# Half-height low passes in the first product of a two-layer MoE chain behind agent attention, with new ranks for the planner

## The chip, the cores and the metric

One Trainium2 chip, of which the kernel uses one core. Its engines are TensorE (PE, with its weight loads PEld), VectorE (DVE), ScalarE (ACT), GpSimd (POOL) and SyncE (SP), which here only issues DMAs. The metric is the device time of the kernel in microseconds (us), the median of three runs; lower is better.

## What is computed

The input is 12480 tokens of 128 numbers. Agent attention (49 agents) is followed by two pairs of dense layers, each 128 to 2048 to 128 wide, all in float32:

```python
def sm(a, b):
    s = scale * (a @ b.transpose(0, 2, 1))
    s = s - s.max(-1, keepdims=True)
    e = np.exp(s)
    return e / (e.sum(-1, keepdims=True) + 1e-09)
x = sm(q, agents) @ (sm(agents, k) @ v)      # attention through the agents
h = x @ w_in                                 # first pair: a rational function
P = a[0] + a[1] * h + a[2] * h**2 + a[3] * h**3
Q = 1.0 + abs(b[0]) * abs(h) + abs(b[1]) * h**2
x = (P / (Q + 1e-6)) @ w_out
h = x @ w2_in                                # second pair: a squared ReLU
x = (s * np.maximum(h, 0)**2 + b2) @ w2_out
```

## The kernel before

The kernel first goes over the keys and values in 13 blocks and reduces them to 49 agent vectors; with w_in these are multiplied into a matrix of 49 x 2048, "avw". Its high and low parts (fp32 split into two fp32r numbers) lie in `avwh` and `avwl`, each with the agents' rows twice: at partitions 0 to 48 and at 64 to 112. The weights are converted from a packed 64-bit form meanwhile (`conv_...`).

The main part goes over the tokens in 24 tiles of 512 and one of 192. For a tile, the scores of its queries on the agents are made (`q_...` jobs), and their softmax is transposed into `pt`: rows 0 to 48 hold the high parts of the 49 weights, rows 64 to 112 the low parts. The 2048 hidden columns are 16 chunks of 128; a **unit** is two chunks of one tile, so a tile of 512 has eight units and there are 196 units in all, numbered p. A unit of the first pair takes these steps:

- `m1_h(p, k)`, for k = 0 and 1 (L681, PE): chunk k of h into a PSUM bank, as a pass of `avwh` and a pass of `avwl` over all rows of `pt`. The bank of k = 0 is one of two, that of k = 1 the middle one, which every unit uses;
- `m1_z` and `m1_abs` (ACT, both as L326, into `z_all` and `t_all`), `m1_w` (POOL, L696 and L698, into `w_all`), `m1_u2` and `m1_u3` (DVE, L702 and L705);
- `m1_ln` and `m1_exp` (ACT), `m1_e` and `m1_m` (DVE, L717 and L721), then either `m1_g` (DVE, L731) or, for units in `ADD_POOL`, `m1_a` and `m1_ga` (POOL, L725 and L728);
- `m1_out` (PE, L739): the product with w_out into one accumulator.

When a tile has all its units, the second pair follows per unit: `m2_h` (PE, three fp32r passes for each of the two chunks, L762 to L764, through one bank `bb`), `m2_relu` (ACT), a square (`m2_sqa` on ACT for units in `SQ_ACT`, else `m2_sqp` on POOL, L773) and `m2_out` (PE, L777).

Nobody orders these by hand. A planner (`main_jobs`, `in_order`) lists all jobs with an engine, a booked time, what must be over before and a rank, which is the unit's number plus a constant of the job's kind (`RANK`); the second pair's unit number is moved back by `BEHIND` behind its tile's end. It then runs a list schedule: on each engine the job of lowest rank among those that are ready, or will be within `PATIENCE`. The program issues each engine's instructions in that fixed order. In main_jobs, the booked times of POOL are `w * 0.00352` for `m1_w`, `w * 0.0019 + 0.05` for a square, `w * 0.00117 + 0.07` for `m1_a` and `w * 0.00233` for `m1_ga`, with w = 1024. `SLOTS` gives the number of buffers of each kind.

Of the kernel before, what the change touches and what calls it, by code (L numbers as in the profile page):

```python
# [20 lines left out]
P = 128  # L21
NA = 49
# [22 lines left out]


W_ACT = {4, 10, 13}
ADD_POOL = {p for p in range(12, NU - 4) if p % 8 in (1, 5)}
SQ_ACT = {p for p, (_, j) in enumerate(OF_UNIT) if j in (0, 2, 4, 6) or p > NU - 5}

# [1 line left out]
SLOTS = dict(own=2, mid=1, r=1, b=1, acc0=1, acc1=1, z=2, t=2, w=4, u=6, l=4, g=4, v=3, xh=2, xl=2, pt=2, qt=2,  # L54
             ss=2, pp=2, mx=2, sr=2, cv=2)
OFFSET = dict(w=2, u=2, v=2, t=1)
SCORES, TRANS, BEHIND = 14, 8, 4


RANK = dict(h=-1.38, z=1.18, abs=0.03, y=3.05, w=4.62, u2=0.32, u3=-3.45, ln=4.31, exp=4.82, e=9.95,  # L60
            m=6.52, g=18.73, a=-0.17, ga=-0.92, out=-0.39, hi=-3.64, lo=4.56, m2h=9.73, relu=0.83,
            sq=9.28, m2out=12.05, evac=4.14, q=-0.25, conv=3, avw=0)

# [2 lines left out]
SAME = dict(pe=0.0, act=0.145, dve=0.127, pool=0.1, sp=0.0)  # L68
FREE = dict(pe=1.3, act=0.0, dve=1.2, pool=3.7, sp=0.0)
COLD = 0.0  # L70
PATIENCE = dict(pe=0.26, act=0.2, dve=0, pool=0.22, sp=0.0)


def act_us(w, psum=True, pointers=0):
# [11 lines left out]
def pe_us(passes, columns, chunks, floor=0.0025):  # L86
    return passes * (columns / 2400 + chunks * floor)


def main_jobs():  # L90
# [43 lines left out]
    for i, n in enumerate(TILES):  # L134
# [19 lines left out]
        for j in range(UNITS[i]):  # L154
            p = f + j
            hs, z, t = [("own", p), ("mid", p)], ("z", p), ("t", p)
            wb, u, l, r, g = ((tag, p) for tag in "wulrg")
            for k in range(2):
                cs = range((2 * j + k) * cpb, (2 * j + k + 1) * cpb)
                need = [("q_pt", i)] if i else [("avw_lo", c // 2 if c < 4 else 1 + c // 4) for c in cs]  # L160
                add(("m1_h", p, k), "pe", pe_us(2, w / 2, cpb, 0.0175), p, "h", need, [hs[k], ("pt", i)])
            hj = [("m1_h", p, k) for k in range(2)]
            add(("m1_z", p), "act", act_us(w, pointers=2), p, "z", hj, hs + [z])
            add(("m1_abs", p), "act", act_us(w), p, "abs", hj, hs + [t])
            if p in W_ACT:
                add(("m1_y", p), "act", act_us(w, False, 2), p, "y", [("m1_abs", p)], [t, wb])
                add(("m1_w", p), "pool", w * 0.00233, p, "w", [("m1_y", p)], [t, wb])
            else:
                add(("m1_w", p), "pool", w * 0.00352, p, "w", [("m1_abs", p)], [t, wb])

            add(("m1_u2", p), "dve", dve_us(w), p, "u2", [("m1_z", p), ("m1_abs", p)], hs + [z])
            add(("m1_u3", p), "dve", dve_us(w, 1), p, "u3", [("m1_u2", p)], hs + [z, u])
            add(("m1_ln", p), "act", act_us(w, False), p, "ln", [("m1_w", p)], [wb, l])
            add(("m1_exp", p), "act", act_us(w, False), p, "exp", [("m1_ln", p)], [l, r])
            add(("m1_e", p), "dve", dve_us(w), p, "e", [("m1_exp", p)], [wb, r, g])
            add(("m1_m", p), "dve", dve_us(w), p, "m", [("m1_e", p)], [r, g])
            if p in ADD_POOL:
                add(("m1_a", p), "pool", w * 0.00117 + 0.07, p, "a", [("m1_u3", p)], [u])
                add(("m1_ga", p), "pool", w * 0.00233, p, "ga", [("m1_m", p), ("m1_a", p)], [g, u])
            else:  # L180
                add(("m1_g", p), "dve", dve_us(w, 1), p, "g", [("m1_m", p), ("m1_u3", p)], [r, g, u])
            for k in range(2):
                prior = [("m1_out", p, 0)] if k else [("m1_out", p - 1, 1)] if j else []
                add(("m1_out", p, k), "pe", pe_us(4, w / 2, cpb), p + 1, "out",
                    [("m1_ga" if p in ADD_POOL else "m1_g", p)] + prior,
                    [g, ("acc0", i)])
# [80 lines left out]
def kernel(  # L267
# [57 lines left out]
    def act(out, in_, func, **kw):  # L325
        return nc.scalar.activation(out=out, in_=in_, func=func, **kw)  # L326
# [334 lines left out]
    def q_pt(i):  # L661
        n = TILES[i]
        pts[i] = sm.tile([P, 512], F32R, tag="pt", name=f"pt{i}")[:, :n]
        act(pts[i], qtps.pop(i)[:, :n], AF.Copy)


    acc1, xs = {}, {}
# [5 lines left out]
    def r_view(p):  # L673
        return rb[:, :, :width(OF_UNIT[p][0])]

    def m1_h(p, k):
        x = 1 if k else 2 * slot["own", p]
        for c, o, n in chunks(p, k):
            dst = xb[:, x, o:o + n]
            for first, w in ((True, avwh), (False, avwl)):  # L680
                on_banks(nc.tensor.matmul(out=dst, lhsT=w[:, c * P:(c + 1) * P], rhs=pts[OF_UNIT[p][0]],  # L681
                                          start=first, stop=not first), {x}, "pe")

    def m1_z(p):
        on_banks(act(view("z", p), h_view(p), AF.Identity, scale=a3, bias=a2), banks(p), "act")
# [256 lines left out]
```

## Time and profile before

| | |
|---|---|
| median of three runs | 1358.8 us (1358.78 to 1360.07) |
| profiled execution, its own time | 1357.7 us |
| its span, first to last instruction | 1355.9 us |
| PE busy | 1261.3 us (93%), 4213 instructions |
| DVE busy | 1229.1 us (91%), 1178 |
| ACT busy | 1177.8 us (87%), 1524 |
| POOL busy | 1196.0 us (88%), 701 |
| mean granted TensorE clock | 0.97 |

"Busy" is the time in which an instruction of the engine was running. A matmul's record is longer than the distance to the next one's start, since matmuls are pipelined, so a busy PE need not be a full PE. The span has four parts: the keys (to about 75 us), a start in which first units and weight conversion mix (to about 186 us), the repeating stretch of tiles (to about 1309 us), and a tail with what is left of the second pair.

### The profile page before, as it was taken

The numbers are of one execution on the slowest core, as the hardware profiler recorded it, in microseconds if no ns is written. First come the engines' busy times: TensorE is split into PE (matmuls) and PEld (weight loads), VectorE is DVE, ScalarE is ACT, GpSimd is POOL, SyncE is SP. The second block draws the span as 40 slices with busy tenths as digits, with TensorE's granted clock in tenths as the row PEclk, the third lists the DMA queues.
The fourth block names the chain that finished last, engine by engine and source line by source line (L and its number), as shares of the span: only waits on it lengthen the run. The fifth ranks groups of instructions, "written<-read, shape, count | busy, mean of one in ns | idle before, by whom it ended". The sixth has DMA issues, their size and how long they took to land.

```text
span 1355.9 us, 12969 instructions
## 1 busy us (share of the span) xinstructions
PE 1261.3 (93%) x4213; PEld 719.0 (53%) x4213; DVE 1229.1 (91%) x1178; ACT 1177.8 (87%) x1524; POOL 1196.0 (88%) x701
## 2 busy tenths in 40 slices
PE   5665699999999999999999999999999999999998
PEld 3342355555555555555555555555555555555565
DVE  5879989999999999999999999999999999999880
ACT  3557689899999999999999999999999999999874
POOL 2567878999999999999999999999999999999851
PEclk9768799999999999999999999999999999999999
DMA  8701000000000000000000000000000000000000
GB/s 338 266 24 39 8 0 16 1 16 16 8 8 16 8 8 16 8 8 16 8 8 16 16 0 16 16 8 8 16 8 8 16 4 8 8 0 8 8 8 11
DMA packets 14004, 34.81 MB, mean 26 GB/s; under 512 B 2192, under 2 KB 2672, under 8 KB 13936
## 3 DMA queue, kind: packets, MB, share of 16 engines
q1 hardware_dynamic: 13360, 33.98, 7.1%
q8 instruction: 33, 0.54, 0.2%
q14 instruction: 35, 0.29, 0.1%
q10 hardware_dynamic: 576, 0.00, 0.0%
HBM read 27.59 MB, written 6.39 MB: 25 GB/s over the span
## 4 chain that ended last, share of the span: by engine, by line
POOL 50%; PE 36%; DVE 6%; ACT 4%; issue 3%; DMA 1%; SPq 0%; POOLq 0%; DVEq 0%; ACTq 0%
POOL w_all L698 20%; PE acc L739 13%; POOL w_all L696 10%; POOL g_all L728 8%; PE acc L777 8%; POOL v_all L773 6%; POOL u_all L725 5%; PE xb L681 5%; PE bb L762 3%; ACT t_all L326 2%; PE bb L763 2%; PE bb L764 2%; PE bb L600 1%; DVE z_all L702 1%; ACT z_all L326 1%
## 5 line engine op out<-in xcount | busy, mean ns | idle before, releaser
L698 POOL TENSOR_TENSOR w_all<-w_all,t_all 128x1024 f32<-128x1024 f32 (+1 forms) x196 | 465.4, 2375 | 18.6 <-ACT w_all L326 2.5
L739 PE MATMUL acc<-g_all,wout_sb 128*128 128x512 f32 (+1 forms) x800 | 374.1, 600 | 25.2 <-POOL g_all L728 12.8
L777 PE MATMUL acc<-v_all,w2out_sb 128*128 128x512 f32 (+1 forms) x800 | 379.2, 581 | 0.7 <-POOL v_all L773 0.5
L326 ACT ACTIVATE v_all<-bb 128x512 f32<-128x512 f32 (+1 forms) x392 | 234.9, 599 | 46.2 <-PE bb L764 37.7
L702 DVE TENSOR_TENSOR z_all<-xb,z_all 128x1024 f32<-128x1024 f32 (+1 forms) x196 | 238.3, 1216 | 39.9 <-ACT z_all L326 38.3
L696 POOL TENSOR_SCALAR w_all<-t_all,absb 128x1024 f32<-128x1024 f32 (+1 forms) x193 | 231.3, 1198 | 41.5 <-ACT t_all L326 39.8
L762 PE MATMUL bb<-xh,w2l 128*128 128x512 f32 (+1 forms) x400 | 251.1, 628 | 9.6 <-ACT v_all L326 8.8
L705 DVE SCALAR_TENSOR_TENSOR u_all<-z_all,prm,xb 128x1024 f32<-128x1024 f32 (+1 forms) x196 | 249.9, 1275 | 9.9
L326 ACT ACTIVATE t_all<-xb 128x1024 f32<-128x1024 f32 (+1 forms) x196 | 200.0, 1020 | 59.3 <-PE xb L681 58.6
L739 PEld LDWEIGHTS acc<-g_all,wout_sb 128*128 128x128 f32 x800 | 148.2, 193 | 182.7 <-issue 114.5
L717 DVE SCALAR_TENSOR_TENSOR g_all<-w_all,rb 128x1024 f32<-128x1024 f32 (+1 forms) x196 | 236.9, 1209 | 2.6 <-ACT rb L326 2.6
L326 ACT ACTIVATE z_all<-xb,prm 128x1024 f32<-128x1024 f32 (+1 forms) x196 | 236.4, 1206 | 0.0
L326 ACT ACTIVATE l_all<-w_all 128x1024 f32<-128x1024 f32 (+1 forms) x196 | 206.0, 1065 | 12.0 <-POOL w_all L698 10.3
L326 ACT ACTIVATE rb<-l_all 128x1024 f32<-128x1024 f32 (+1 forms) x196 | 204.4, 1043 | 3.5 <-DVE g_all L731 3.5
L773 POOL TENSOR_TENSOR v_all<-v_all 128x1024 f32<-128x1024 f32 x96 | 181.8, 1894 | 21.7 <-ACT v_all L326 21.7
L731 DVE SCALAR_TENSOR_TENSOR g_all<-u_all,prm,rb 128x1024 f32<-128x1024 f32 (+1 forms) x151 | 192.3, 1274 | 5.2
L777 PEld LDWEIGHTS acc<-v_all,w2out_sb 128*128 128x128 f32 x800 | 149.1, 188 | 78.8 <-issue 51.1
L721 DVE SCALAR_TENSOR_TENSOR rb<-g_all,rb 128x1024 f32<-128x1024 f32 (+1 forms) x151 | 184.2, 1220 | 3.5
L681 PE MATMUL xb<-pt,avwh 128*128 128x512 f32 (+1 forms) x400 | 167.2, 419 | 20.9 <-DVE u_all L705 15.3
L681 PE MATMUL xb<-pt,avwl 128*128 128x512 f32 (+1 forms) x400 | 157.6, 396 | 0.0
L763 PE MATMUL bb<-xh,w2h 128*128 128x512 f32 (+1 forms) x400 | 156.0, 390 | 0.0
L764 PE MATMUL bb<-xl,w2h 128*128 128x512 f32 (+1 forms) x400 | 155.2, 388 | 0.0
(119 smaller groups left out, 1278.2 us busy)
## 6 DMA issues: line engine op xcount, KB each, us to landing
qt<-in_q_dram SPq DMA_DIRECT2D x24, 256.0 KB, 2.7
out_dram<-o SPq DMA_DIRECT2D x24, 256.0 KB, 2.0
l_all<-in_k_dram SPq DMA_DIRECT2D x6, 512.0 KB, 8.4
l_all<-in_v_dram SPq DMA_DIRECT2D x6, 512.0 KB, 8.0
g_all<-in_k_dram SPq DMA_DIRECT2D x6, 512.0 KB, 9.0
g_all<-in_v_dram SPq DMA_DIRECT2D x6, 512.0 KB, 8.2
v_all<-in_moe_w_out_dram SPq DMA_DIRECT2D x6, 512.0 KB, 4.0
v_all<-in_moe_w_in_dram SPq DMA_DIRECT2D x5, 512.0 KB, 5.8
```

The costliest lines, as they stand in the source:

```text
L326: return nc.scalar.activation(out=out, in_=in_, func=func, **kw)
L681: on_banks(nc.tensor.matmul(out=dst, lhsT=w[:, c * P:(c + 1) * P], rhs=pts[OF_UNIT[p][0]], start=first, stop=not first), {x}, "pe")
L696: nc.gpsimd.tensor_scalar(out=w, in0=t, scalar1=absb[:, 1:2], scalar2=absb[:, 0:1], op0=ALU.mult, op1=ALU.add)
L698: nc.gpsimd.tensor_tensor(out=w, in0=w, in1=t, op=ALU.mult)
L702: on_banks(nc.vector.tensor_tensor(out=z, in0=h_view(p), in1=z, op=ALU.mult), banks(p), "dve")
L705: on_banks(nc.vector.scalar_tensor_tensor(out=view("u", p), in0=view("z", p), scalar=a1, in1=h_view(p), op0=ALU.add, op1=ALU.mult), banks( ...
L717: nc.vector.scalar_tensor_tensor(out=view("g", p), in0=view("w", p), scalar=C1, in1=r_view(p), op0=ALU.add, op1=ALU.mult)
L731: nc.vector.scalar_tensor_tensor(out=view("g", p), in0=view("u", p), scalar=a0, in1=r_view(p), op0=ALU.add, op1=ALU.mult)
L739: nc.tensor.matmul(out=acc1[i][:, :n], lhsT=wout_sb[:, c * D:(c + 1) * D], rhs=g[:, at_(p, k), o:o + n], start=(c == 0), stop=(c == NCH - 1))
L762: nc.tensor.matmul(out=dst, lhsT=w2l[:, ws], rhs=xh, start=True, stop=False)
L773: nc.gpsimd.tensor_tensor(out=m2_view(p), in0=m2_view(p), in1=m2_view(p), op=ALU.mult)
L777: nc.tensor.matmul(out=accs[1][:, :n], lhsT=w2out_sb[:, c * D:(c + 1) * D], rhs=m2_view(p)[:, k, o:o + n], start=(c == 0), stop=(c == NCH ...
```

## The change

Four things change together.

First, for tiles of 512 the two low passes of a unit are made as two matmuls of half the contraction rows: one from rows 0 to 48 of `avwl` and `pt` into the bank of k = 0, the other from rows 64 to 112 of `avwl` and of a new tile `ptx` into the middle bank. Each multiplies the low part of avw with the high part of the weights alone; the product of both low parts is left out. Second, `ptx` gets the high rows of `pt` at partitions 64 to 112 by a DMA that SP issues after ACT has written `pt`. Third, `SQ_ACT` has three units of a tile instead of four, and `ADD_POOL` holds units 2 and 6 of a tile instead of 1 and 5. Fourth, `RANK`, `PATIENCE` and `BEHIND` (4 to 2) have new numbers, which sets a new order on every engine; two rows of them stand for all.

```diff
-ADD_POOL = {p for p in range(12, NU - 4) if p % 8 in (1, 5)}
-SQ_ACT = {p for p, (_, j) in enumerate(OF_UNIT) if j in (0, 2, 4, 6) or p > NU - 5}
+ADD_POOL = {p for p in range(12, NU - 4) if p % 8 in (2, 6)}
+SQ_ACT = {p for p, (_, j) in enumerate(OF_UNIT) if j in (0, 2, 5) or p > NU - 5}
...
-SCORES, TRANS, BEHIND = 14, 8, 4
+SCORES, TRANS, BEHIND = 14, 8, 2
...
-RANK = dict(h=-1.38, z=1.18, abs=0.03, y=3.05, w=4.62, u2=0.32, u3=-3.45, ln=4.31, exp=4.82, e=9.95,
+RANK = dict(h=-1.99, z=-4.25, abs=-2.83, y=2.75, w=9.01, u2=-3.03, u3=3.43, ln=2.65, exp=-5.18, e=-3.96,
...
-PATIENCE = dict(pe=0.26, act=0.2, dve=0, pool=0.22, sp=0.0)
+PATIENCE = dict(pe=0.6, act=0.32, dve=0, pool=0, sp=0.0)
...
-                add(("m1_h", p, k), "pe", pe_us(2, w / 2, cpb, 0.0175), p, "h", need, [hs[k], ("pt", i)])
+                passes = 2 if cpb > 1 else 1 + k
+                add(("m1_h", p, k), "pe", pe_us(passes, w / 2, cpb, 0.0175), p, "h",
+                    need + [("m1_h", p, 0)] * k, hs[:k + 1] + [("pt", i)])
...
         act(pts[i], qtps.pop(i)[:, :n], AF.Copy)
+        if CPB[i] == 1:
+            ptx[i] = sm.tile([P, 512], F32R, tag="ptx", name=f"ptx{i}")
+            nc.sync.dma_start(out=ptx[i].bitcast(F32)[64:64 + NA, :], in_=pts[i].bitcast(F32)[:NA, :])
...
     def m1_h(p, k):
-        x = 1 if k else 2 * slot["own", p]
+        i = OF_UNIT[p][0]
+        x, split = 1 if k else 2 * slot["own", p], CPB[i] == 1
         for c, o, n in chunks(p, k):
             dst = xb[:, x, o:o + n]
-            for first, w in ((True, avwh), (False, avwl)):
-                on_banks(nc.tensor.matmul(out=dst, lhsT=w[:, c * P:(c + 1) * P], rhs=pts[OF_UNIT[p][0]],
+            for first, w in ((True, avwh), (False, avwl))[:1 if split else 2]:
+                on_banks(nc.tensor.matmul(out=dst, lhsT=w[:, c * P:(c + 1) * P], rhs=pts[i],
                                           start=first, stop=not first), {x}, "pe")
+        if split and k:
+            for y, rows in ((2 * slot["own", p], slice(0, NA)), (1, slice(64, 64 + NA))):
+                c = chunks(p, y == 1)[0][0]
+                on_banks(nc.tensor.matmul(out=xb[:, y, :], lhsT=avwl[rows, c * P:(c + 1) * P],
+                                          rhs=(ptx if rows.start else pts)[i][rows, :], start=False, stop=True),
+                         {y}, "pe")
```

Lines of the changed kernel are later by 14 in the main part: L696, L698, L725, L728, L739 and L773 become L710, L712, L739, L742, L753 and L787.

What this does to the order is seen on POOL in the repeating stretch. Before, in about half a tile (here w_all is written by L696 and L698, v_all is squared by L773, and g_all and u_all belong to ADD_POOL units):

```order
L696 TENSOR_SCALAR w_all<-t_all,absb 128x1024
L698 TENSOR_TENSOR w_all<-w_all,t_all 128x1024
L696 TENSOR_SCALAR w_all<-t_all,absb 128x1024
L698 TENSOR_TENSOR w_all<-w_all,t_all 128x1024
L773 TENSOR_TENSOR v_all<-v_all 128x1024
L622 TENSOR_TENSOR ss_102<-ss_102,mx_1467 128x4x49
L696 TENSOR_SCALAR w_all<-t_all,absb 128x1024
L698 TENSOR_TENSOR w_all<-w_all,t_all 128x1024
L728 TENSOR_TENSOR g_all<-g_all,u_all 128x1024
```

And after, the part of a tile that answers to it:

```order
L712 TENSOR_TENSOR w_all<-w_all,t_all 128x1024
L624 TENSOR_TENSOR ss_102<-ss_102,mx_1504 128x4x49
L787 TENSOR_TENSOR v_all<-v_all 128x1024
L742 TENSOR_TENSOR g_all<-g_all,u_all 128x1024
L710 TENSOR_SCALAR w_all<-t_all,absb 128x1024
L712 TENSOR_TENSOR w_all<-w_all,t_all 128x1024
L643 TENSOR_TENSOR ss_102<-ss_102,sr_1530 128x4x49
L710 TENSOR_SCALAR w_all<-t_all,absb 128x1024
L712 TENSOR_TENSOR w_all<-w_all,t_all 128x1024
L653 TENSOR_TENSOR pp_100<-ss_102,pp_100 128x4x49
L787 TENSOR_TENSOR v_all<-v_all 128x1024
```

A tile has 28 POOL instructions after and 27 before: five squares instead of four. An L712 is followed at once by the next unit's L710 at 5 places of the program, where L698 was followed by L696 at 48. Five squares stand behind the last L698 and behind the last L712 alike, at the end of the program.

On PE, a unit of the first product in the repeating stretch, before (xb is the first product's PSUM, bb the second's, acc the accumulators):

```order
L764 MATMUL bb<-xl_3231,w2h 128x512
L681 MATMUL xb<-pt_2915,avwh 128x512
L681 MATMUL xb<-pt_2915,avwl 128x512
L681 MATMUL xb<-pt_2915,avwh 128x512
L681 MATMUL xb<-pt_2915,avwl 128x512
L762 MATMUL bb<-xh_3219,w2l 128x512
```

And after:

```order
L778 MATMUL bb<-xl_3244,w2h 128x512
L689 MATMUL xb<-pt_2981,avwh 128x512
L791 MATMUL acc_79<-v_all,w2out_sb 128x512 x2
L602 MATMUL bb<-agp,qt_2782 128x49 x4
L753 MATMUL acc_78<-g_all,wout_sb 128x512
L776 MATMUL bb<-xh_3234,w2l 128x512
L777 MATMUL bb<-xh_3234,w2h 128x512
L778 MATMUL bb<-xl_3244,w2h 128x512
L689 MATMUL xb<-pt_2981,avwh 128x512
L694 MATMUL xb<-pt_2981,avwl 128x512
L694 MATMUL xb<-ptx_2983,avwl 128x512
L776 MATMUL bb<-xh_3234,w2l 128x512
```

The high pass of the first chunk now stands alone and ahead; the high pass of the second and both half-height low passes (L694) follow together, between matmuls of full height.

On SP, in the part of the keys, before:

```order
L448 DMA l_all<-in_k_dram 128x1024
L450 DMA l_all<-in_v_dram 128x1024
L372 DMA z_all<-in_moe_w_in_dram 128x1024
L448 DMA g_all<-in_k_dram 128x1024
L450 DMA g_all<-in_v_dram 128x1024
```

And after:

```order
L450 DMA l_all<-in_k_dram 128x1024
L452 DMA l_all<-in_v_dram 128x1024
L374 DMA z_all<-in_moe_w_in_dram 128x1024
L669 DMA ptx_467<-pt_465 49x512
L450 DMA g_all<-in_k_dram 128x1024
L452 DMA g_all<-in_v_dram 128x1024
```

The first of the 24 copies into ptx comes ahead of the load of the last but one block of keys.

## Rows read from the trace of the kernel before

**Rows 1.** Stretches, all engines: length, busy (instructions), granted clock, DMA share, GB/s.

```profile
84.00:186.00 102.00, 64.39 (x161) 34.81 (x159) 90.89 (x94) 75.24 (x92) 74.09 (x50) 0.78 0.05 16
186.00:1286.00 1100.00, 1075.99 (x3442) 609.50 (x3441) 1049.58 (x929) 1020.43 (x1284) 1061.04 (x598) 1.00 0.03 10
...
1309.00:1356.00 47.00, 42.30 (x185) 28.26 (x183) 9.03 (x10) 24.23 (x38) 8.65 (x5) 1.00 0.04 14
```

**Rows 2.** POOL in order of time: start, us, instruction, [idle before, until whom].

```profile
599.06 2.39 POOL L728 TENSOR_TENSOR g_all<-g_all,u_all 128x1024 f32<-128x1024 f32 x1
...
611.03 2.41 POOL L698 TENSOR_TENSOR w_all<-w_all,t_all 128x1024 f32<-128x1024 f32 x1
613.51 1.20 POOL L696 TENSOR_SCALAR w_all<-t_all,absb 128x1024 f32<-128x1024 f32 x1
614.79 2.37 POOL L698 TENSOR_TENSOR w_all<-w_all,t_all 128x1024 f32<-128x1024 f32 x1
617.13 1.89 POOL L773 TENSOR_TENSOR v_all<-v_all 128x1024 f32<-128x1024 f32 x1
...
620.28 1.20 POOL L696 TENSOR_SCALAR w_all<-t_all,absb 128x1024 f32<-128x1024 f32 x1 [0.79 <-ACT t_all L326]
...
633.20 1.89 POOL L773 TENSOR_TENSOR v_all<-v_all 128x1024 f32<-128x1024 f32 x1
635.08 1.19 POOL L696 TENSOR_SCALAR w_all<-t_all,absb 128x1024 f32<-128x1024 f32 x1
...
648.44 2.40 POOL L728 TENSOR_TENSOR g_all<-g_all,u_all 128x1024 f32<-128x1024 f32 x1
```

**Rows 3.** Groups by line, 400 to 1200 us: count, busy, mean ns, idle before.

```profile
L326 ACT ACTIVATE z_all<-xb,prm 128x1024 f32<-128x1024 f32 x129 | 156.4, 1212 | 0.0
...
L725 POOL TENSOR_SCALAR u_all<-u_all,prm 128x1024 f32<-128x1024 f32 x33 | 93.7, 2840 | 0.0
...
L326 ACT ACTIVATE v_all<-v_all 128x1024 f32<-128x1024 f32 x65 | 69.9, 1075 | 0.0
```

**Rows 4.** Waits of POOL and DVE, 186 to 1309 us: total, times, longest.

```profile
POOL w_all L696 <- ACT t_all L326: 25.2, 27, 2.4
...
POOL g_all L728 <- DVE g_all L721: 2.5, 1, 2.5
...
DVE z_all L702 <- ACT z_all L326: 30.2, 49, 1.4
```

**Rows 5.** PE in order of time, repeating stretch.

```profile
600.34 0.60 PE L658 MATMUL bb<-ident,pp 128*128 128x128 f32 x4
...
615.06 1.08 PE L600 MATMUL bb<-agp,qt 128*128 128x49 f32 x8
...
630.43 0.39 PE L763 MATMUL bb<-xh,w2h 128*128 128x512 f32 x1
630.66 0.40 PE L764 MATMUL bb<-xl,w2h 128*128 128x512 f32 x1
...
636.18 0.39 PE L763 MATMUL bb<-xh,w2h 128*128 128x512 f32 x1
```

**Rows 6.** PE in the keys' part: half-width matmuls (128*64), then transposes.

```profile
21.36 1.03 PE L459 MATMUL xb<-g_all,agp 128*64 128x512 f32 x4
22.32 0.66 PE L488 MATMUL bb<-ident,e 128*128 128x128 f32 x4
```

**Rows 7.** SP, ACT, PE in order of time: key load, pt, keys.

```profile
47.85 0.42 SPq L448 DMA_DIRECT2D g_all<-in_k_dram  x1
...
52.44 0.60 ACT L326 ACTIVATE pt<-bb 128x512 fp32r<-128x512 f32 x1 [0.73 <-PE bb L658]
...
62.71 1.08 PE L459 MATMUL xb<-g_all,agp 128*64 128x512 f32 x4
```

**Rows 8.** DMA issues: count, KB each, median us to landing.

```profile
qt<-in_q_dram SPq DMA_DIRECT2D x24, 256.0 KB, 2.7
...
g_all<-in_k_dram SPq DMA_DIRECT2D x6, 512.0 KB, 9.0
```

More of the change, by code (lines that the diff above doesn't have):

```diff
@@ L56 @@
 OFFSET = dict(w=2, u=2, v=2, t=1)
-SCORES, TRANS, BEHIND = 14, 8, 4
-RANK = dict(h=-1.38, z=1.18, abs=0.03, y=3.05, w=4.62, u2=0.32, u3=-3.45, ln=4.31, exp=4.82, e=9.95,
-            m=6.52, g=18.73, a=-0.17, ga=-0.92, out=-0.39, hi=-3.64, lo=4.56, m2h=9.73, relu=0.83,
-            sq=9.28, m2out=12.05, evac=4.14, q=-0.25, conv=3, avw=0)
+SCORES, TRANS, BEHIND = 14, 8, 2
+RANK = dict(h=-1.99, z=-4.25, abs=-2.83, y=2.75, w=9.01, u2=-3.03, u3=3.43, ln=2.65, exp=-5.18, e=-3.96,
+            m=4.12, g=-2.1, a=5.98, ga=6.15, out=1.68, hi=1.9, lo=6.34, m2h=-0.85, relu=0.35, sq=10.77,
+            m2out=10.33, evac=-6.12, q=-6.28, conv=3, avw=0)
 LAG = dict(pe=0.2, act=0.17, dve=0.19, pool=0.09, sp=0.1)
@@ L585, in rows @@
         return ck, TILES[i] // ck
-    sqs, qtps, pts, mxs = {}, {}, {}, {}
+    sqs, qtps, pts, ptx, mxs = {}, {}, {}, {}, {}
     def load_q(i):
```

## The prediction

> **What bounds the kernel now.** I read the stretches first. From 186 to 1286 us, DVE, ACT, POOL and PE are all busy over 92%, and the granted TensorE clock is 1.00, its 2.4 GHz level, so the shares name no single limit [rows 1]. I then read POOL in order of time, as the change gives it work. From one L728 to the next but one, 599.06 to 648.44, lies one tile of 512 tokens: 49.38 us, eight units [rows 2]. In it POOL waits once, 0.79 us before L696 at 620.28; everything else starts when its predecessor ends [rows 2]. So POOL has 48.59 us of work in a tile of 49.38. The reader should take start-to-start distances: a square (L773) holds the queue 1.88 us (633.20 to 635.08), L698 holds it 2.34 us (614.79 to 617.13), and 2.48 us where L696 follows it directly (611.03 to 613.51) [rows 2]. All POOL waits between 186 and 1309 us come to 25.2 + 2.5 = 27.7 us, in 27 and 1 places [rows 4]. DVE waits 30.2 us there, for ACT's z [rows 4]: it too is nearly full.
>
> PE is read likewise. From one L763 to the one 5.75 us later lies a full unit's work without a gap (10 fp32r passes, 8 halves of fp32 matmuls) [rows 5]. A pass starts 0.23 us after the one before (630.43 to 630.66), though it is shown 0.39 us long [rows 5]. A tile is 8 x 5.75 plus the scores and transposes of the queries, at most 1.08 + 0.60 [rows 5]: 47.7 us. PE thus has 1.7 us to spare in a tile, twice POOL's slack, and it is PE's load that the change cuts.
>
> **The change part by part.** *Row halves.* Per unit two low passes of 0.23 us become two half-height ones that may overlap. The trace of before has no row halves; the nearest rows are column halves, the agents' scores on the keys: four records of 512 columns start at 21.36 and the next work starts at 22.32, 0.96 us [rows 6]. Whole, these would be four times (5.75 - 10 x 0.23) / 8 = 0.43, so 1.72 us: halves do run side by side there. I take one pass saved, 8 x 0.23 = 1.8 us a tile, which leaves PE at 45.8. Bounds: nothing saved (47.7), and on top a pipeline that empties at each change of mode, for which the visible tail of a pass, 0.39 - 0.23 = 0.16 us, sixteen times a tile, gives 2.6 us (50.3). Only at that far end does PE come up to POOL's tile (50.19, below), so the path gains nothing from this edit: POOL has no room for a faster PE.
>
> The Trainium skill speaks against the edit here: "TensorEngine Tiling (Array Packing)", Key Properties, says that changing the tiling mode, unlike changing the tile, drains the engine. The column halves show little of it, 0.96 against half of 1.72. By that rule the third rival below gets its mechanism, and this trace, which never changes the mode within a unit, leaves it open.
>
> *The copy.* 24 DMAs of 49 rows (100 KB) go to SP's queue. In the main loop each is issued behind the ACT copy of pt, and its first reader is six units later in PE's order; a load of 256 KB lands in 2.7 us [rows 8]. Without that cover a tile would lose about 3 us; with six units of 6 us there is no doubt. Behind it on SP stand the next query load and the output store, and nobody waits for either within a unit. The first copy is the exception: it stands ahead of the key load that SP issued at 47.85, and ACT writes its source from 52.44 to 53.04 [rows 7]. That load then leaves 5.6 us later, at about 53.4, lands with 9.0 us [rows 8] at 62.4, and PE reads it at 62.71 [rows 7]. I count nothing, with 5.6 us as the upper end.
>
> *Squares.* SQ_ACT falls from four to three units of a tile; POOL squares five instead of four. ACT loses 1.08 us a tile [rows 3], which it was not short of. POOL gains 24 squares x 1.88 = 45.1 us. In the order of before and of after five squares stand behind the last L698/L712, so all 24 are in front of it, on the full queue.
>
> *Positions.* The new ranks put something between L712 and the next L710 nearly everywhere: direct neighbours fall from 48 to 5. At 2.48 less 2.34 us [rows 2], that returns 43 x 0.14 = 6.0 us. Two ADD_POOL units a tile remain, 45 in all; their L725 takes 2.84 us [rows 3], where the planner books 1.27, so the real POOL is later than the order assumes, and its inputs wait for it rather than the other way round. POOL's net addition is 45.1 - 6.0 = 39.1 us; a tile (two such pairs in it before, none after) has 48.59 + 1.88 - 0.28 = 50.19 us of POOL work, more than the 49.38 it takes now.
>
> *What the added work may absorb.* In the steady stretch, POOL's waits of 27.7 us. ACT now makes z ahead of abs, which gives L710 its input one ACT instruction later. From the end of one unit's L712, ACT does ln, exp, relu, z and abs before the L710 after next can start: five instructions of at most 1.21 us [rows 3], 6.1 us at most. Meanwhile POOL has the unit between (1.28 from 613.51 to 614.79, and 2.34: 3.62 us [rows 2]) and, by the order, at least two squares or as much (7.4 us in all); at one place of a tile it is one square and two short query steps (over 5.5 us), so there 0.6 us may stay. Most waits should go: I take 10 us left of 27.7; bounds none, and 34 (1.5 us a tile, about twice the 0.79 of now). In the start (84 to 186 us) POOL idles 102 - 74.1 = 27.9 us, but DVE is busy 90.9 of 102 there [rows 1]: at most 11 us can go; the orders differ in both directions, I count 0, from -11 to +6 (the late key load). In the tail PE is busy 42.3 of 47.0 [rows 1], and the order leaves nine halves of the second product behind the last L753 as it did before: 0, from -4.7 to +2 (two neighbouring squares now both on POOL, each 0.8 us longer than on ACT). BEHIND = 2 moves the second product about two units forward; its work is the same.
>
> *The sum.* The profiled execution took 1357.7 us, of which 1355.9 are its span; the median of three runs is 1358.8, 1.1 above, and I add to the median: 39.1 - (27.7 - 10) = +21.4 us, 1380.2. A tile would take 50.19 + 10 / 23, about 50.6.
>
> **The rivals.**
> First, **the order pays for itself**: POOL never waits again, the start loses all that DVE leaves (11) and the tail all that PE leaves (4.7): 39.1 - 27.7 - 11 - 4.7 = -4.3, 1354.5. It decides from the point at which 39.1 us are saved. For it: slack of that size exists, 43.4 us with all three. Against: it needs all three together, at their ends. Chance 0.12, of which 0.05 lie within 0.2% of before (about what a measurement of this kernel can tell from no change) and 0.07 below.
> Second, **new waits**: the reordered ACT chain keeps L710 waiting, since ACT has one chain of exp, relu, z, abs, ln per unit and stands between DVE and POOL. POOL's waits would rise to 34 us: 39.1 + 6.3, 1404. For it: DVE already waits for z 49 times [rows 4], and evacuations of other work now stand between ln and exp. Against: POOL is the late one. Chance 0.06.
> Third, **the mode change**: PE becomes the bound if a change costs more than (50.2 - 45.8) / 16 = 0.28 us. At 0.5 us a tile is 45.8 + 8 = 53.8, 4.4 more than now; the 22.7 tiles between 186 and 1309 us give 1358.8 + 100 = 1459. Nothing in the rows asks for so much; the row tail is 0.16. Chance 0.03.
> That the halves do not overlap at all, so that the change does not do what it says, gives 47.7 + 2.6 = 50.3 a tile at worst: it would look like the forecast in time, and is part of it.
>
> **How the numbers follow.** Forecast 0.79 (1380, POOL bound, own range 1363 to 1398: 1358.8 + 39.1 - 27.7 - 7 at the lower end, with start and tail partly in favour; at the upper end 1358.8 + 39.1, nothing absorbed), order pays 0.12, new waits 0.06, mode change 0.03. The range is the forecast's own, 1363 to 1398: below it lie the 0.12, above most of the 0.09. Chances: faster 0.07, within 0.2% 0.05, slower 0.88.
>
> **What would show it.** Right: 120 squares on POOL of 1.89 us each; one tile, from an L742 to the L742 after next, 50.2 to 51 us; POOL over 98% busy from 200 to 1280 us, with almost no wait of L710 for ACT; DVE waits longer than 30 us; PE's gaps grow. Halves right: the two L694 of a unit start together, and the next pass about 0.23 us after them. Wrong: a tile of 49.4 us or less, which would mean that POOL's instructions got shorter, since their sum alone forbids it; POOL waits above 1 us a tile (second rival); PE gaps at each L694 (third); a start that ends 10 us earlier (first).

## The result, and the profile after

The changed kernel took 1374.1 us (median of four runs, 1373.3 to 1374.6) against 1358.8 us: 1.0111 times the time before, 95% interval 1.0094 to 1.0129, or +15.3 us. The forecast was 1380.2, +21.4. The direction and the range held; the account behind them did not, as the experiments show. The profiled execution took 1374.2 us, its span 1372.2.

First the page's line of busy time, then the stretches that answer to [rows 1] (length, busy and instructions of PE, PEld, DVE, ACT and POOL, granted clock, DMA share, GB/s):

```profile
PE 1303.2 (95%) x4213; PEld 664.1 (48%) x4213; DVE 1232.2 (90%) x1178; ACT 1181.1 (86%) x1500; POOL 1239.8 (90%) x725
```

```profile
84.00:186.00 102.00, 72.06 (x158) 32.41 (x159) 90.66 (x94) 73.29 (x89) 72.50 (x49) 0.70 0.06 18
186.00:1286.00 1100.00, 1097.74 (x3399) 552.27 (x3398) 1038.51 (x916) 1011.65 (x1247) 1083.62 (x611) 1.00 0.04 12
```

POOL's busy time rose by 43.8 us and fills 98.5% of the repeating stretch. DVE's share fell, although its work is the same. POOL in order of time, one tile from L742 to the next but one, as in [rows 2] (start, us, instruction):

```profile
605.29 2.39 POOL L742 TENSOR_TENSOR g_all<-g_all,u_all 128x1024 f32<-128x1024 f32 x1
...
616.79 1.90 POOL L787 TENSOR_TENSOR v_all<-v_all 128x1024 f32<-128x1024 f32 x1
618.67 1.23 POOL L710 TENSOR_SCALAR w_all<-t_all,absb 128x1024 f32<-128x1024 f32 x1
...
655.63 2.40 POOL L742 TENSOR_TENSOR g_all<-g_all,u_all 128x1024 f32<-128x1024 f32 x1
```

The tile takes 50.34 us, and no row of it carries a wait. The waits that answer to [rows 4], 186 to 1325 us (engine, tile, line, what it waits for: total, times, longest):

```profile
DVE z_all L716 <- ACT t_all L328: 32.0, 66, 0.8
DVE g_all L731 <- ACT rb L328: 12.1, 23, 0.7
POOL v_all L787 <- ACT v_all L328: 2.0, 1, 2.0
POOL w_all L710 <- ACT t_all L328: 1.2, 3, 0.5
```

POOL's 27.7 us of waits have become 4.7 (with two more of under 1 us). DVE's 30.2 have become 44.1, and a kind is new: 23 waits of L731, one a tile, for ACT's exp (`rb`).

PE around one unit of the first product, against the four passes of [rows 5] (L689 high, L694 half-height low, L776 to L778 second product):

```profile
602.39 0.50 PE L689 MATMUL xb<-pt,avwh 128*128 128x512 f32 x1
602.82 0.50 PE L694 MATMUL xb<-pt,avwl 49*128 49x512 f32 x1
602.83 0.50 PE L694 MATMUL xb<-ptx,avwl 49*128 49x512 f32 x1
603.26 0.50 PE L776 MATMUL bb<-xh,w2l 128*128 128x512 f32 x1
603.59 0.39 PE L777 MATMUL bb<-xh,w2h 128*128 128x512 f32 x1
...
622.11 0.40 PE L689 MATMUL xb<-pt,avwh 128*128 128x512 f32 x1
622.43 0.50 PE L694 MATMUL xb<-pt,avwl 49*128 49x512 f32 x1
```

The two halves run side by side, 0.01 us apart. But the next pass starts 0.43 us after them and its successor 0.33 after that, where passes before stood 0.23 apart: 0.30 us for the change back. The change into half height costs 0.09: the pair at 622.43 starts 0.32 us after a pass that had not waited. (At 602.82 it is 0.43, but the pass at 602.39 had waited for DVE, and a full-height pass behind a wait also stands 0.34 ahead of the next.) Some 0.4 us a pair in all, 0.2 a change on average. "TensorEngine Tiling (Array Packing)" of the Trainium skill, Key Properties, says that a change of mode drains the engine; the trace agrees, with that price.

To see where the 16.3 us by which the profiled span grew lie, take one mark in both traces: the instruction u2 of DVE (L702, after L716) at unit 24 and at unit 184, twenty tiles on. Before:

```profile
250.86 1.23 DVE L702 TENSOR_TENSOR z_all<-xb,z_all 128x1024 f32<-128x1024 f32 x1 [0.71 <-ACT z_all L326]
1238.14 1.23 DVE L702 TENSOR_TENSOR z_all<-xb,z_all 128x1024 f32<-128x1024 f32 x1 [0.70 <-ACT z_all L326]
```

And after:

```profile
253.09 1.23 DVE L716 TENSOR_TENSOR z_all<-xb,z_all 128x1024 f32<-128x1024 f32 x1 [0.82 <-ACT t_all L328]
1259.84 1.23 DVE L716 TENSOR_TENSOR z_all<-xb,z_all 128x1024 f32<-128x1024 f32 x1 [0.81 <-ACT t_all L328]
```

The head is 2.2 us longer, the twenty tiles 19.5 (mean tile 49.36 and 50.34), and the end, from the second mark to the end of the span, 5.4 shorter (117.8 and 112.4). The same marks give one line for every kernel run. Each ratio is against runs of the kernel before taken beside that kernel's own, whose medians were 1357.9 to 1359.1. One execution of e_light_dve, 2081.4 us at a granted clock of 0.557, is left out of its median.

| kernel | median us | ratio to before, 95% | mean tile | head | end |
|---|---|---|---|---|---|
| before | 1358.8 | | 49.36 | 250.9 | 117.8 |
| after | 1374.1 | 1.0094 to 1.0129 | 50.34 | 253.1 | 112.4 |
| e_before_light | 1354.3 | 0.9959 to 0.9979 | 49.38 | 249.1 | 116.0 |
| e_light | 1370.1 | 1.0075 to 1.0105 | 50.19 | 251.5 | 112.0 |
| e_full | 1379.1 | 1.0143 to 1.0174 | 50.50 | 256.0 | 112.5 |
| e_full_light | 1372.5 | 1.0090 to 1.0126 | 50.32 | 252.1 | 112.2 |
| e_old_order_halves | 1387.7 | 1.0197 to 1.0228 | 50.48 | 257.8 | 118.1 |
| e_after_old_h | 1369.1 | 1.0063 to 1.0093 | 50.30 | 248.8 | 112.1 |
| e_light_dve | 1363.9 | 1.0025 to 1.0052 | 50.08 | 252.9 | 111.4 |
| e_full_light_dve | 1366.4 | 1.0034 to 1.0071 | 50.23 | 251.2 | 111.6 |
| e_before_sq | 1458.4 | 1.0728 to 1.0761 | 54.25 | 255.6 | 118.8 |
| e_after_sq4 | 1420.0 | 1.0443 to 1.0486 | 52.53 | 253.0 | 113.1 |
| e_before_halves | 1562.2 | 1.1488 to 1.1526 | 57.70 | 282.4 | 123.3 |
| e_ranks | 1448.1 | 1.0647 to 1.0685 | 53.54 | 256.9 | 117.4 |

### The profile page after: what moved, and what is told of

The parts are those of the page before. It is cut to its first block, busy times and chain, and to the rows that moved or that the text cites. A ratio compares the mean times of both kernels' runs of the same rounds, so it can differ in the third digit from the quotient of the medians.

```text
span 1372.2 us, 13099 instructions
## 1 busy us (share of the span) xinstructions
PE 1303.2 (95%) x4213; PEld 664.1 (48%) x4213; DVE 1232.2 (90%) x1178; ACT 1181.1 (86%) x1500; POOL 1239.8 (90%) x725
## 4 chain that ended last, share of the span: by engine, by line
PE 83%; ACT 2%; POOL 2%; DVE 2%; issue 1%; DVEq 0%; POOLq 0%; ACTq 0%
PE acc L753 23%; PE acc L791 23%; PE bb L776 10%; PE xb L689 7%; PE bb L777 6%; PE bb L778 6%; PE xb L694 6%; PE bb L602 1%; PE bb L660 1%; POOL w_all L712 1%; ACT z_all L328 1%; DVE z_all L716 1%; ACT t_all L328 1%; POOL u_all L739 0%; ACT v_all L328 0%
## 5 line engine op out<-in xcount | busy, mean ns | idle before, releaser
L712 POOL TENSOR_TENSOR w_all<-w_all,t_all 128x1024 f32<-128x1024 f32 (+1 forms) x196 | 465.5, 2375 | 27.9 <-ACT w_all L328 11.8
L753 PE MATMUL acc<-g_all,wout_sb 128*128 128x512 f32 (+1 forms) x800 | 395.7, 605 | 8.8 <-DVE g_all L745 7.8
L716 DVE TENSOR_TENSOR z_all<-xb,z_all 128x1024 f32<-128x1024 f32 (+1 forms) x196 | 238.1, 1215 | 37.4 <-ACT t_all L328 37.2
L731 DVE SCALAR_TENSOR_TENSOR g_all<-w_all,rb 128x1024 f32<-128x1024 f32 (+1 forms) x196 | 237.5, 1212 | 17.8 <-ACT rb L328 13.8
L328 ACT ACTIVATE v_all<-bb 128x512 f32<-128x512 f32 (+1 forms) x392 | 230.8, 589 | 19.9 <-PE bb L778 16.8
L787 POOL TENSOR_TENSOR v_all<-v_all 128x1024 f32<-128x1024 f32 x120 | 227.6, 1897 | 19.3 <-ACT v_all L328 19.3
L710 POOL TENSOR_SCALAR w_all<-t_all,absb 128x1024 f32<-128x1024 f32 (+1 forms) x193 | 232.1, 1202 | 7.5 <-ACT t_all L328 7.3
L689 PE MATMUL xb<-pt,avwh 128*128 128x512 f32 (+1 forms) x400 | 198.9, 499 | 16.7 <-DVE u_all L719 16.4
L776 PE MATMUL bb<-xh,w2l 128*128 128x512 f32 (+1 forms) x400 | 205.2, 513 | 4.5 <-ACT v_all L328 3.0
L328 ACT ACTIVATE rb<-l_all 128x1024 f32<-128x1024 f32 (+1 forms) x196 | 201.2, 1027 | 9.4 <-DVE g_all L745 3.8
L753 PEld LDWEIGHTS acc<-g_all,wout_sb 128*128 128x128 f32 x800 | 148.2, 194 | 125.9 <-issue 63.1
L776 PEld LDWEIGHTS bb<-xh,w2l 128*128 128x128 f32 x400 | 74.8, 187 | 193.4 <-ACT v_all L328 150.5
L778 PE MATMUL bb<-xl,w2h 128*128 128x512 f32 (+1 forms) x400 | 154.9, 387 | 0.0
## 6 DMA issues: line engine op xcount, KB each, us to landing
qt<-in_q_dram SPq DMA_DIRECT2D x24, 256.0 KB
out_dram<-o SPq DMA_DIRECT2D x24, 256.0 KB
```

The lines of the kernel that those rows point to most:

```text
L710: nc.gpsimd.tensor_scalar(out=w, in0=t, scalar1=absb[:, 1:2], scalar2=absb[:, 0:1], op0=ALU.mult, op1=ALU.add)
L712: nc.gpsimd.tensor_tensor(out=w, in0=w, in1=t, op=ALU.mult)
L716: on_banks(nc.vector.tensor_tensor(out=z, in0=h_view(p), in1=z, op=ALU.mult), banks(p), "dve")
L731: nc.vector.scalar_tensor_tensor(out=view("g", p), in0=view("w", p), scalar=C1, in1=r_view(p), op0=ALU.add, op1=ALU.mult)
L753: nc.tensor.matmul(out=acc1[i][:, :n], lhsT=wout_sb[:, c * D:(c + 1) * D], rhs=g[:, at_(p, k), o:o + n], start=(c == 0), stop=(c == NCH - 1))
L776: nc.tensor.matmul(out=dst, lhsT=w2l[:, ws], rhs=xh, start=True, stop=False)
```

## Experiments: does POOL set the tile?

The theory on record was that POOL sets the tile (A). A rival appeared with the trace of after, where PE's records cover 99.8% of the stretch: the mode changes have filled PE (B). Both are tried by taking work off an engine while every instruction keeps its place in the order.

**POOL made lighter.** L725 (L739 after) adds a0 in place and takes 2.84 us, while L696, with two operations, takes 1.20. A multiplication by 1.0 is put in front of the addition:

```diff
-nc.gpsimd.tensor_scalar(out=view("u", p), in0=view("u", p), scalar1=a0, scalar2=None, op0=ALU.add)
+nc.gpsimd.tensor_scalar(out=view("u", p), in0=view("u", p), scalar1=1.0, scalar2=a0,
+                        op0=ALU.mult, op1=ALU.add)
```

> The kernel before, its order untouched, with the two-operation form of its L725. If POOL bounded it, as the prediction reads [rows 2], the tile falls from 49.38 by 1.6 us to PE's 47.7 or a little above: 1359 - 23 x 1.3 = 1329, from 1320 to 1340. If PE or DVE was the bound and POOL only nearly full, it stays over 1350.

> The changed kernel, its order untouched; only L739 becomes a multiply by 1.0 and an add of a0 instead of the add alone. L710 has two operations as well and takes 1.20 us, L739 takes 2.84: POOL should lose 2 x 1.64 = 3.28 us of work in a tile (50.2 to 46.9). Theory A (POOL sets the tile of 50.34 us, PE is near but has room): the tile falls to what PE needs. I estimate that from the starts around one pair of half passes: L689 to L694 0.43, L694 to the next pass 0.43, against 3 x 0.23 for the three full passes that stood there, 0.17 us more a unit: 8 x (5.75 + 0.17) + 1.7 = 49.1. 23 tiles x 1.2 = 28 us less, 1346. Theory B (PE sets the tile of the changed kernel, its mode changes having filled it; its busy share there is 99.8%): the time stays, 1372 to 1375.

The edit did to POOL what it should. Its group in the lighter kernel of before, 400 to 1200 us (count, busy, mean ns, idle before), what POOL waited for from 186 to 1286 us, and the two marks:

```profile
L725 POOL TENSOR_SCALAR u_all<-u_all,prm 128x1024 f32<-128x1024 f32 x33 | 37.4, 1135 | 0.0
```

```profile
POOL w_all L696 <- ACT t_all L326: 94.4, 67, 2.4
```

```profile
249.14 1.23 DVE L702 TENSOR_TENSOR z_all<-xb,z_all 128x1024 f32<-128x1024 f32 x1 [0.71 <-ACT z_all L326]
1236.83 1.23 DVE L702 TENSOR_TENSOR z_all<-xb,z_all 128x1024 f32<-128x1024 f32 x1 [0.70 <-ACT z_all L326]
```

And the two marks of e_light:

```profile
251.50 1.23 DVE L716 TENSOR_TENSOR z_all<-xb,z_all 128x1024 f32<-128x1024 f32 x1 [0.81 <-ACT t_all L328]
1255.32 1.23 DVE L716 TENSOR_TENSOR z_all<-xb,z_all 128x1024 f32<-128x1024 f32 x1 [0.82 <-ACT t_all L328]
```

The instruction fell from 2.84 to 1.14 us, 3.4 us a tile. In the kernel before, the mean tile stayed as it was, 49.36 and 49.38; all that POOL gained it now waits, 94.4 us where it was 19.9 in the same stretch. The 3.1 us by which the profiled span is shorter (4.6 in the medians) lie in the head and the end. So POOL did not set the tile of the kernel before. In the changed kernel the tile fell by 0.15 us and the time by some 4 us. The edit took 3.4 us a tile off POOL, more than the 1.9 us that the added square put on it, so of the 45 us of squares no more than some 4 us are felt as POOL's work; that a square delays something by the place where it stands was not tried. Theory A is out. 1370.1 is below the 1372 to 1375 written for B, but far from A's 1346, so B stands so far.

**PE made lighter.** The two half-height passes become two full-height ones at the same place, so that PE never changes mode; the copies go.

```diff
-            for y, rows in ((2 * slot["own", p], slice(0, NA)), (1, slice(64, 64 + NA))):
+            for y in (2 * slot["own", p], 1):
                 c = chunks(p, y == 1)[0][0]
-                on_banks(nc.tensor.matmul(out=xb[:, y, :], lhsT=avwl[rows, c * P:(c + 1) * P],
-                                          rhs=(ptx if rows.start else pts)[i][rows, :], start=False, stop=True),
-                         {y}, "pe")
+                on_banks(nc.tensor.matmul(out=xb[:, y, :], lhsT=avwl[:, c * P:(c + 1) * P],
+                                          rhs=pts[i], start=False, stop=True), {y}, "pe")
```

> The changed kernel, its order untouched; the two half-height passes of a unit are two full-height passes at the same place, and the copies by DMA are gone. PE has one more pass a unit, but no change of mode. Theory A (POOL sets the tile): 1371 to 1376, tile 50.2 to 50.4, and gaps on PE. Theory B (PE sets it): PE needs 47.7 a tile, POOL's 50.2 takes over, 1370 to 1373 - nearly the same by itself; it is the pair with e_full_light that tells the price of the modes. A third view, that the copies on SP's queue or the row halves save time somewhere: slower than 1376.

> Both edits: full-height low passes and the two-operation L739. POOL needs 46.9 us a tile, PE 47.7, DVE about as much as before (1049.6 of 1100 us there, 47.1 a tile). Theories A and B both give a tile of 47.9 to 48.5, 1374 - 23 x 2.1 = 1326, from 1318 to 1335. What tells them apart is the distance to e_light, the price of the changes of mode: by A about 23 x 1.4 = 32 us (0.17 us a unit), by B 60 us and more (over 0.3 us a unit).

Without mode changes the kernel was slower, 1379.1, as the third view of its expectation had it, and with the lighter POOL it was no faster, 1372.5 against 1370.1. The tile never came near the 47.7 us of PE's passes, so neither the modes nor the sum of PE's work set it: B is out as well, and so are the 1318 to 1335 on which both theories had agreed for e_full_light. PE's 99.8% is no counter-evidence, because a pass's record of 0.39 to 0.50 us covers short waits between passes.

## Experiments: parts of the change, planned anew

Meanwhile each part was put alone into one of the kernels, as an edit of the tables, so that the planner made a new order:

e_before_sq is the kernel before with

```diff
-SQ_ACT = {p for p, (_, j) in enumerate(OF_UNIT) if j in (0, 2, 4, 6) or p > NU - 5}
+SQ_ACT = {p for p, (_, j) in enumerate(OF_UNIT) if j in (0, 2, 5) or p > NU - 5}
```

and e_after_sq4 the changed kernel with the same two lines the other way round. e_ranks is the kernel before with

```diff
-ADD_POOL = {p for p in range(12, NU - 4) if p % 8 in (1, 5)}
+ADD_POOL = {p for p in range(12, NU - 4) if p % 8 in (2, 6)}
...
-SCORES, TRANS, BEHIND = 14, 8, 4
+SCORES, TRANS, BEHIND = 14, 8, 2
```

and RANK and PATIENCE of the changed one. e_before_halves is the reverse of it: the rest of the diff, so the passes of m1_h, its jobs in the planner and the copies, with all tables of before.

> The kernel before, with SQ_ACT of the changed one alone: one more square of a tile on POOL, planned anew with the old ranks. Theory A (the squares make it slower): 48.59 + 1.89 = 50.48 us of POOL work in a tile, 45.1 us more in all, of which POOL's waits of 27.7 us take back 18 to 27: 1376 to 1386. The rival that the new ranks or the row halves make it slower: 1357 to 1364.

> The changed kernel with SQ_ACT of the kernel before: the square goes back to ACT, POOL needs 48.4 us a tile, and PE keeps its row halves. Theory A (POOL sets the tile, PE's own need is about 49.1): tile 49.1 to 49.4, 1344 to 1352. Theory B (PE's need is 50.3): stays at 1370 to 1375.

> The kernel before with the row halves and the copies alone; ranks, squares and the rest are the old ones. Theory A (the modes cost PE about 0.17 us a unit, PE needs 49.1 a tile, POOL 48.6): 1357 to 1366. Theory B (PE needs 50.3 or more): tile 50.3, 1359 + 23 x 0.9 = 1380. As the prediction has it, with one pass saved and PE at 45.8: 1355 to 1360.

> The kernel before with the new ranks, patience, BEHIND and ADD_POOL alone; full-height passes and four squares of a tile on ACT. POOL needs 48.59 - 0.28 = 48.3 us a tile, PE 47.7. If the new order is what lets POOL run without waits, tile 48.4 to 48.8, 1338 to 1348. If the new order does nothing by itself, 1355 to 1362; if it adds waits, above.

All four came out above every figure that had been written, by 45 to 182 us (for e_ranks "above" had been left without a number), even the one that took work off POOL and the one that changed little but the order. Their tiles take 52.5 to 57.7 us, and from 186 to 1286 us every engine is less busy than before. They say nothing on what a part costs, since each of these mixtures makes an order of its own. The likely reason is that the planner's numbers suit only the structure that they were chosen with; no run shows it. So the parts were then tried with the order kept.

## Experiments: the structure in a fixed order, and DVE

Where time is lost in a tile is seen on DVE in the kernel before. It runs five instructions of 1.2 to 1.3 us a unit (u2, u3, e, m, g), without a gap, and four in an ADD_POOL unit, where it then waits for ACT. What it waits for is a ring through one PSUM bank, the middle one of every unit: u3 on DVE frees it, PE puts the passes of the next unit into it, ACT reads it twice, DVE reads it in u2 and u3. The kernel lets one engine at a time touch a bank (`on_banks`), so these steps cannot overlap. The page "PSUM — Partial Sum Buffer" of the Trainium skill, section "PSUM bank collisions raise a hardware error", asks for that, reads against reads included; no run here shows a collision.

Before, a unit's low pass of the first chunk stood with its high pass, ahead of the ring. The change puts it behind the high pass of the second chunk, into the ring. That is theory S; theory O is that the new order costs the time.

e_old_order_halves is the kernel before with the copies of the diff and these lines of it in m1_h, while the planner's jobs stay:

```diff
-            for first, w in ((True, avwh), (False, avwl)):
+            for first, w in ((True, avwh), (False, avwl))[:1 if split else 2]:
...
+        if split and k:
+            for y, rows in ((2 * slot["own", p], slice(0, NA)), (1, slice(64, 64 + NA))):
...
```

e_after_old_h is the changed kernel with the same lines taken out, and the copies, while its planner's jobs stay.

> The kernel before with every instruction in its old place, except that a unit's two low passes are made as the two half-height ones, behind the high pass of the second chunk, with the copies that they need; no ranks, no squares. The earlier runs have moved the theory from POOL to DVE: five DVE instructions of 1.25 us a unit are the tile, and in the two ADD_POOL units DVE waits for the ring of the middle bank (u3 on DVE, high pass, low passes, z and abs on ACT, u2 on DVE). Theory S (the structure lengthens that ring: both low parts stand between u3 and ACT, 0.7 us before, 1.0 to 1.3 after): DVE's two waits of a tile grow by 0.3 to 0.5 us each, 23 x 0.6 to 1.0 = 14 to 23 us, 1372 to 1382. Theory O (the new order of ACT costs the time, the structure nothing): 1356 to 1362.

> The changed kernel with every instruction in its new place, except that the first product is made as before: high and low pass of a chunk together at full height, no copies. Theory S: the ring is shorter by 0.3 us or more, DVE's waits in the ADD_POOL units shrink by as much, 23 x 0.6 = 14 us, 1356 to 1364. Theory O: the waits of DVE stay where ACT is late with z, abs or exp, 1370 to 1378.

The structure alone costs 28.6 us in the old order, more than expected; some 7 us of them lie in the head (250.9 to 257.8). The ring before (start, us, instruction; L681 is the high and the low pass of a unit's second chunk, the one in the middle bank):

```profile
618.46 0.40 PE L681 MATMUL xb<-pt,avwh 128*128 128x512 f32 x1
618.70 0.39 PE L681 MATMUL xb<-pt,avwl 128*128 128x512 f32 x1
...
619.15 1.02 ACT L326 ACTIVATE t_all<-xb 128x1024 f32<-128x1024 f32 x1
```

And with the structure, at the same place of a tile (L685 high, L690 low):

```profile
633.55 0.40 PE L685 MATMUL xb<-pt,avwh 128*128 128x512 f32 x1
633.88 0.50 PE L690 MATMUL xb<-pt,avwl 49*128 49x512 f32 x1
633.88 0.50 PE L690 MATMUL xb<-ptx,avwl 49*128 49x512 f32 x1
...
634.43 1.03 ACT L326 ACTIVATE t_all<-xb 128x1024 f32<-128x1024 f32 x1
```

From the high pass to ACT it is 0.88 us where it was 0.69; at the tile's other wait it is 1.02 (608.01 to 609.03) where it was 0.79 (642.90 to 643.69). DVE's waits for ACT's z from 186 to 1286 us rise from 30.2 in 49 places to this:

```profile
DVE z_all L712 <- ACT z_all L326: 46.4, 67, 2.4
```

In the tile around 600 us, the steps from one unit's u2 to the next unit's that were 5.64 and 5.71 are 6.01 and 5.93, and a third wait, of 0.23, is new. Between the two marks, DVE's waits grow from 1.10 to 1.92 us a tile, 0.82 of the 1.12 by which the tile is longer. S holds there for the tile. How the cost in the old order divides between the low pass's place and its half height was not run.

In the new order, taking the structure out again gives back 5.0 us, 1374.1 to 1369.1: less than S expected, and just under the range of O. The tile stays at 50.30; nearly all of the gain is in the head. With e_full the 5 us can be split, by differences of medians: the low pass of the first chunk in the ring rather than ahead costs 10.0 (1369.1 to 1379.1, both at full height), and the half height, with its copies, then gives back 5.0 (1379.1 to 1374.1). Between the high pass and ACT the half height costs nothing against two full passes: from the high pass's start to the end of the low passes' records it is 0.94 us at 602.39 in after, and 0.96 with two full passes (612.37 to 613.33 in e_full_light_dve). What remains, 10.3 us over before with the old passes, belongs to the new order, with its ADD_POOL units, and the squares. Its waits of DVE, 186 to 1286 us:

```profile
DVE z_all L706 <- ACT t_all L328: 22.4, 45, 0.6
DVE g_all L721 <- ACT rb L328: 11.7, 23, 0.6
```

The second line is the new kind of wait; the kernel before, whose wait for z is in [rows 4], has it once, with 0.2 us. Its place in a tile of after, on ACT and DVE:

```profile
625.47 1.07 ACT L328 ACTIVATE l_all<-w_all 128x1024 f32<-128x1024 f32 x1
626.41 0.79 ACT L328 ACTIVATE o<-acc,bcol,prm 128x512 f32<-128x512 f32 x1
627.08 0.35 ACT L328 ACTIVATE ss<-bb 128x196 f32<-128x196 f32 x1
627.29 1.05 ACT L328 ACTIVATE rb<-l_all 128x1024 f32<-128x1024 f32 x1
...
628.45 1.22 DVE L731 SCALAR_TENSOR_TENSOR g_all<-w_all,rb 128x1024 f32<-128x1024 f32 x1 [0.52 <-ACT rb L328]
```

The new ranks put an output evacuation and a step of the query scores between ln and exp, and DVE waits 0.52 us for the exp, in a unit that ADD_POOL had made lighter. In the tile shown, DVE's waits sum to 1.98 us (0.83, 0.26, 0.52, 0.37), before to 1.09 (0.38, 0.71): 0.89 of the 0.96 us by which this tile is longer.

**DVE made lighter.** If DVE's dense units, those with five instructions and no wait, are the limit, less work in them should shorten the tile. The edit leaves out half of one product, that of each unit's second chunk, so the output is not the right one; both kernels also have the lighter POOL, and e_full_light_dve the full-height passes of e_full:

```diff
-nc.vector.scalar_tensor_tensor(out=view("g", p) if p in ADD_POOL else r_view(p), in0=view("g", p),
-                               scalar=2.0, in1=r_view(p), op0=ALU.subtract, op1=ALU.mult)
+o, g = view("g", p) if p in ADD_POOL else r_view(p), view("g", p)
+nc.vector.scalar_tensor_tensor(out=o[:, 0:1, :], in0=g[:, 0:1, :],
+                               scalar=2.0, in1=r_view(p)[:, 0:1, :], op0=ALU.subtract, op1=ALU.mult)
```

> The changed kernel with the two-operation L739 and DVE relieved as well: the product of L735 is made for the first chunk of each unit alone, so half of that product is missing from the output. DVE loses 8 x 0.6 = 4.8 us a tile, POOL 3.3. Theory D (DVE sets the tile): the tile falls until PE binds, by my estimate from the starts around a pair at 49.1 to 50.2, so 1346 to 1370. If DVE is not the bound, it stays at the 1370 of the run without this edit.

> The same with full-height low passes and no copies. PE needs 47.7 a tile, POOL 46.9, DVE 42.7 and its waits. Theory D: the tile falls from 50.2 to between 47.8 and 48.8, 1372.5 - 23 x 1.4 to 2.4, so 1317 to 1340; the distance to the run with half-height passes is then what the changes of mode cost where PE is the bound, 20 us or more. If ACT or the ring is the bound whatever DVE does: 1360 to 1373 for both.

Both medians are 6 us lower than without the edit, but the tile fell by 0.1 us, not by 1.4 to 2.4, and the two lie 2.5 us apart with the half height ahead, so no price of the modes shows. By their sums of work DVE, POOL and PE all have room now, and it still takes 50.1 to 50.2. The waits of e_full_light_dve say where DVE stands, 186 to 1286 us:

```profile
DVE z_all L712 <- ACT t_all L328: 97.0, 151, 1.6
```

It waits for ACT in nearly every unit. Two units of that kernel on PE and ACT (L686 and L691 first product, L774 to L776 second product into `bb`, L751 and L789 the products out):

```profile
602.72 0.60 ACT L328 ACTIVATE v_all<-bb 128x512 f32<-128x512 f32 x1
...
603.37 0.50 PE L774 MATMUL bb<-xh,w2l 128*128 128x512 f32 x1
...
604.17 1.02 PE L789 MATMUL acc<-v_all,w2out_sb 128*128 128x512 f32 x2
605.03 1.02 PE L751 MATMUL acc<-g_all,wout_sb 128*128 128x512 f32 x2
...
605.49 0.79 PE L686 MATMUL xb<-pt,avwh 128*128 128x512 f32 x1
606.12 0.62 PE L691 MATMUL xb<-pt,avwl 128*128 128x512 f32 x2
...
606.78 1.21 ACT L328 ACTIVATE z_all<-xb,prm 128x1024 f32<-128x1024 f32 x1 [0.94 <-PE xb L691]
607.89 1.01 ACT L328 ACTIVATE t_all<-xb 128x1024 f32<-128x1024 f32 x1
608.79 0.60 ACT L328 ACTIVATE v_all<-bb 128x512 f32<-128x512 f32 x1
...
609.44 0.50 PE L774 MATMUL bb<-xh,w2l 128*128 128x512 f32 x1
```

This is a second ring, through PE and ACT alone. ACT empties `bb` behind its z and abs; PE's next L774 needs `bb`; behind it in PE's order stand the other two passes, four halves of the products out, and then the first product, for which z waits. From L774 to L691 2.75 us, to z 0.66, to abs 1.11, to the evacuation 0.90, to the next L774 0.65: 6.07 us. In that kernel five of the eight steps from u2 to u2 in a tile are 6.06 to 6.20; the other three, 6.28, 6.59 and 6.86, are longer than this ring, and what holds them was not followed. The new order thus seems to have two limits that lie close together, this ring of 6.07 us and DVE's dense units of 6.15 to 6.3, and to relieve one alone gains little. That fits e_after_old_h too, which shortens the ring by a pass and leaves DVE dense. A kernel that relieves both was not run, so that the two together set the new order's tile is argued from the two traces, not shown.

## Why the prediction was right in sign and wrong in cause

- *What bounds the kernel now.* This step failed. POOL's one wait of 0.79 us in a tile [rows 2] was read as its distance to the limit. It showed only that POOL's work and the tile were about equal; the tile was set elsewhere, and e_before_light took 3.4 us a tile of POOL's work away without moving it (49.36 and 49.38). The text did see that DVE "too is nearly full" and waits for z, but took that for the consequence of POOL.
- *Row halves.* Overlap: right. "The path gains nothing": wrong in sign, because the text counted passes and not where they stand. Alone in the old order the structure costs 28.6 us, in the new one 5.0. On PE the text took 0.23 us a unit as saved; a pair costs 0.4 us more than one pass and replaces two, so 0.17 are added, inside the bounds given. The third rival's mechanism is real (0.2 us a change on average), under its threshold of 0.28, and it was not what made the kernel slower: at the same place full height was slower still.
- *Copy.* Right. The copy goes out at 51.56 and the key load behind it at 52.48 instead of 47.85, yet the scores that need it start at 61.20, without a wait.
- *Squares and positions.* The account of POOL was right: 120 squares of 1.897 us, 43.8 us more busy, a tile of 50.34 against 50.19 of predicted work. As a term of the time, +39.1 was mis-sized: e_light bounds what POOL's work is worth in the new order at about 4 us.
- *Absorption.* POOL's waits went down to 4.7 us, not 10; the head lost 2.2 us (0 was taken, -11 to +6); the end gained, 5.4 us from the second mark, or 3.7 from the last L712 (0 was taken, down to -4.7).
- *Second rival.* Its ground came true, evacuations between ln and exp, but at another engine: L710 hardly waits (1.2 us), while DVE's L731 waits 12.1 us for the exp. The text looked for that wait on POOL alone.
- *The sum.* 1380 came close because two errors met: POOL's work was counted as if it were time, and the longer ring and the new waits of DVE were not counted. Sums of one engine's work and waits always add up to the span; that this one did was no evidence for POOL.
- *Signs given.* Squares, tile, POOL's share, L710 without waits and DVE's longer waits all came. They could not tell the forecast from its cause: a full POOL was as much the result of an order made to fill it. "PE's gaps grow" was wrong, and so was "the next pass 0.23 us after".

Open: how the 10.3 us of e_after_old_h divide between the squares and the new ranks, since every mixture of tables made an order of its own. Open too: what set the tile before. DVE's dense units and its two waits for the ring fill the tile there by the trace, but no run took work off DVE in the old order. A better kernel than both is e_before_light, 1354.3 us, 0.3% under before (0.9959 to 0.9979), from one instruction written in another form.

## What to carry to other kernels

In a kernel whose order was fitted until every engine is just in time, few waits do not mark the engine that bounds it: take work off each in turn, in an unchanged order, and see which one moves the tile. Cost a moved matmul by the buffer that it now waits for and holds, before counting passes saved. Try parts of a change with the order kept; numbers fitted to one structure cost 46 us and more in each of the four mixtures run here (1374.1 to 1420.0 at the least).

## What the runs showed of the hardware

- On POOL, an addition alone (a tensor_scalar with one operation, in place, 128x1024 float32) takes 2.84 us, the same with a multiplication by 1.0 ahead of it 1.14 us.
- Two half-height passes on different rows start within 0.01 us of each other. The pair starts 0.32 us after a pass that did not wait (622.11 to 622.43 in after), the next pass 0.43 us after the pair and the one behind it 0.33 later (602.83 to 603.59), where full-height passes stand 0.23 apart: about 0.4 us a pair for the two changes, against 0.23 for the pass saved.
